# Block-sparse attention and expert routing on one core: gathered blocks interleaved over partitions 32 to 95

## The chip, the cores and the metric

The kernel runs on one core of one Trainium2 chip. A core has a matrix engine (TensorE, PE; its weight loads are PEld), three engines for elementwise work (VectorE or DVE, ScalarE or ACT, GpSimd or POOL), a queue engine that issues transfers (SyncE or SP), and 16 DMA engines. Its fast memory, SBUF, has 128 partitions; results of matrix multiplications go to PSUM. The metric is the device time in microseconds (us) of one execution. A profile is one further execution taken by the hardware profiler; its span runs from the first to the last instruction.

## What is computed

Sparse attention (4 batch entries, 8 heads, 768 positions, head size 64) is followed by a router that sends each token to one of 8 experts. Positions form 24 blocks of 32. A query block sees its own block and the two beside it, the first and the last block, and three blocks drawn at random for it. The first and last query blocks see everything.

```python
scores = scale * np.matmul(q, k.transpose(0, 1, 3, 2))
mask = np.abs(blk_i - blk_j) <= 1
mask = mask | (blk_i == 0) | (blk_j == 0) | (blk_i == n_blocks - 1) | (blk_j == n_blocks - 1)
for qb in range(n_blocks):
    for kb in sampled_blocks[qb]:
        mask[qb * block:(qb + 1) * block, kb * block:(kb + 1) * block] = True
attn = softmax(np.where(mask, scores, -1e9))
x = np.matmul(attn, v)                    # then to (3072 tokens, 512)
...
logits = normalized(x) @ normalized(expert_emb).T / tau
expert_idx = np.argmax(logits, axis=1)    # gate_w: its softmax probability
out[mask_e] = gate_w[mask_e, None] * (np.maximum(x[mask_e] @ w1[e], 0.0) @ w2[e])
```

All data are float32. The random block numbers are an input, so the kernel reads them on the device and uses them as addresses.

## The kernel before

**Stages.** Attention fills about the first 265 us. The rest is the experts: tiles of 128 tokens, whose rows are gathered by an indirect transfer and multiplied by `w1` (L1171) and `w2` (L1184), with 4 MB of weights for each tile.

**Attention.** Two batch entries are taken together (a pair, `DUO`), and the positions are cut into 6 chunks of 128, each with 4 query blocks, g = 0 to 3 (`NG`). One step of the loop in `attention_fast` (25 of them) handles one chunk of one batch entry. The order of the work on every engine is the order in which this loop writes it; no scheduler changes it. The loop is software-pipelined: in step s PE scores chunk s (`score_near`, `score_far`) and weighs the values of chunk s - 1 (`weigh_near`, `weigh_far`), DVE and POOL collect the keys of chunk s + 1 (`gather_k`), and SP issues the transfers of values for a later pair of chunks (`gather_v`).

**Near and far.** Keys that lie together (the window's own pair of blocks, and the first and last block) are multiplied where they are (`score_near`). Four further key blocks of each query block g are collected into one set of 128 lanes: the three random blocks, called slots 0, 1 and 2 (`NRAND`), and one neighbour block. In the keys' tile `kg` the lanes lie along the free dimension, so collecting is a copy within each partition. DVE copies slot 0 and the neighbour (L532, L536), POOL copies slots 1 and 2 (L532). PE then multiplies the lanes in two halves of 64 (L575), ACT takes the exponential with a bias for each lane (L580), which blanks a lane whose block is seen already, and the result `pd` has the lane as its partition. PE therefore needs the values of the same four blocks with the lane as partition, in the tile `vg` (L630). The three random slots of `vg` come from memory by transfers on SP, one for each slot and query block, for both batch entries and all heads at once: 32 rows of 16 pieces of 256 bytes, 128 KB (L469, issued in `fetch_all` at L476, L478 and L480). POOL copies the neighbour from the values that are in SBUF (L490). `vg` has two buffers, used by turns by pairs of chunks.

**Lanes before.** Slot r has lanes 32 r to 32 r + 31, and the neighbour has 96 to 127, in `kg`, `vg` and the bias alike. The bias, one number for each lane and query block, is built once near the start on DVE (`build_bias`, L351 to L370), between a copy of turned keys (L503) and the first collecting copies.

**Queues.** All loads of attention but three go through SP's one queue, in the order written: gathers (vg) with a load of q, k or v ahead of every other one, and the write of finished rows to `x_dram` (L834), from which the experts' tiles gather.

Of the kernel before, what the change touches and what calls it, by code (L numbers as in the profile page):

```python
# [12 lines left out]
F32 = mybir.dt.float32  # L13
I32 = mybir.dt.int32
BF16 = mybir.dt.bfloat16
ACT = mybir.ActivationFunctionType
ALU = mybir.AluOpType
# [3 lines left out]
P = 128  # L21
B, H, S, D = 4, 8, 768, 64
BLK = 32
NB = S // BLK
NRAND = 3
# [26 lines left out]
NI = NB - 2  # L52
# [6 lines left out]
NONE = -30000.0  # L59
# [28 lines left out]
def warm_up(k, times):  # L88

    if k.zeros is None:  # L90
        k.zeros = k.const.tile([P, 512], BF16, name="zeros")
        k.nc.vector.memset(k.zeros, 0.0)
        k.warm = two_banks(k, "warm")
    for i in range(times):
        k.nc.tensor.matmul(k.warm[:, 0], lhsT=k.zeros[:, 0:P], rhs=k.zeros, start=True, stop=True)
# [253 lines left out]
def build_bias(k):  # L349

    nc, pool, r = k.nc, k.setup, k.rand  # L351
    own = pool.tile([P, NI], F32, name="own_block")
    nc.gpsimd.iota(own, pattern=[[1, NI]], base=1, channel_multiplier=0, allow_small_or_imprecise_dtypes=True)
    bad = pool.tile([P, NRAND, NI], F32, name="bad_block")
    nc.vector.tensor_tensor(out=bad, in0=r, in1=own.unsqueeze(1).broadcast_to([P, NRAND, NI]), op=ALU.subtract)
    nc.vector.tensor_tensor(out=bad, in0=bad, in1=bad, op=ALU.mult)
    nc.vector.tensor_scalar(out=bad, in0=bad, scalar1=1.5, scalar2=None, op0=ALU.is_le)
    nc.vector.scalar_tensor_tensor(out=bad, in0=r, scalar=0.5, in1=bad, op0=ALU.is_le, op1=ALU.max)
    nc.vector.scalar_tensor_tensor(out=bad, in0=r, scalar=NB - 1.5, in1=bad, op0=ALU.is_ge, op1=ALU.max)
    for s, t in ((1, 0), (2, 0), (2, 1)):  # L360
        same = pool.tile([P, NI], F32, name=f"same{s}{t}")
        nc.vector.tensor_tensor(out=same, in0=r[:, s], in1=r[:, t], op=ALU.is_equal)
        nc.vector.tensor_tensor(out=bad[:, s], in0=bad[:, s], in1=same, op=ALU.max)
    k.bias = k.const.tile([P, NI], F32, name="bias")
    nc.vector.memset(k.bias, 0.0)
    for i in (0, NI - 1):
        nc.vector.memset(k.bias[NRAND * BLK:P, i:i + 1], NONE)
    for s in range(NRAND):
        lanes = slice(s * BLK, (s + 1) * BLK)
        nc.vector.tensor_scalar(out=k.bias[lanes], in0=bad[lanes, s], scalar1=NONE, scalar2=None, op0=ALU.mult)  # L370


def shifts(k, engine, s, c):

    blocks = blocks_of(c)
    key = engine, s, c
    if key not in k.shift:
        _, values = k.nc.values_load_multi_w_load_instructions(
            k.offset[0:1, s, NG * c + blocks[0]:NG * c + blocks[-1] + 1], engines=(engine,), min_val=0, max_val=S - BLK,
            skip_runtime_bounds_check_because="the block numbers are clamped to the blocks there are")  # L380
        if engine == mybir.EngineType.SP and s == NRAND - 1:
            return list(values)
        k.shift[key] = list(values)
    return k.shift[key]


def pair_chunk(s):

    a, at = divmod(s, NC)
    return a, at if a == 0 else (at + 1) % NC  # L390


def place(n):

    a, c = pair_chunk(n // DUO)
    return DUO * a + n % DUO, c, n % DUO


def of_seq(src, a, i=None):

    if i is None:
        return src[DUO * a:DUO * (a + 1)].rearrange("i h s d -> s (i h) d")
    return src[DUO * a + i].rearrange("h s d -> s h d")


def in_pair(t, i=None):

    return t.rearrange("p i h e -> p (i h) e") if i is None else t[:, i]
# [24 lines left out]
def which(i):  # L433

    return slice(0, DUO) if i is None else slice(i, i + 1)
# [15 lines left out]
def blocks_of(c):  # L451

    return range(2 if c == 0 else 0, NG)


def home(block):

    tile = (block + 1) // 2
    lo = (D if tile % 2 else 0) + BLK * (1 - block % 2)
    return slice(lo, lo + BLK), tile // 2  # L460


def gather_v(k, s, i=None):

    a, c = pair_chunk(s)
    t, src = k.vg_ring[s % 2], of_seq(k.v, a, i)
    for r in range(NRAND):
        for g, shift in zip(blocks_of(c), shifts(k, mybir.EngineType.SP, r, c)):
            yield in_pair(t[r * BLK:(r + 1) * BLK, g], i)[:, :, 0:D], src[bass.ds(shift, BLK)]  # L469


def fetch_all(k, gathers, loads):
# [10 lines left out]
def near_v(k, s, some, i=None):  # L483

    _, c = pair_chunk(s)
    for g in blocks_of(c):
        block = NG * c + g - 2 if g % 2 == 0 else NG * c + g
        if g in some and 0 < block < NB - 1:
            rows, m = home(block)
            k.nc.gpsimd.tensor_copy(out=k.vg_ring[s % 2][NRAND * BLK:P, g, which(i)], in_=k.vt[m][rows, which(i)])  # L490


def turn_k(k, g):
# [28 lines left out]
def gather_k(k, n):  # L522

    nc = k.nc
    b, c, _ = place(n)
    kt = k.kt[b % 2]
    k.kg[n] = t = k.gp.tile([P, NPAIR, NG, P], F32, name="kg", tag="kg")
    for s in range(NRAND):
        engine, copy = ((mybir.EngineType.Pool, nc.gpsimd.tensor_copy) if s else
                        (mybir.EngineType.DVE, nc.vector.tensor_copy))  # L530
        for g, shift in zip(blocks_of(c), shifts(k, engine, s, c)):
            copy(out=t[:, :, g, s * BLK:(s + 1) * BLK], in_=kt[:, :, bass.ds(shift, BLK)])  # L532
    for half in range(1 if c == 0 else 0, 2):
        for z in range(2):
            lo = BLK * (NG * c + 2 * half - 2 + 3 * z)
            nc.vector.tensor_copy(out=t[:, :, 2 * half + z, NRAND * BLK:P], in_=kt[:, :, lo:lo + BLK])  # L536


def score_near(k, n):
# [723 lines left out]
def attention_fast(n, ctx):  # L1263
# [3 lines left out]
    nc = n.nc  # L1267
# [26 lines left out]
        fetch_all(n, (), load_k(n, g))  # L1294
    load_experts(n)
    warm_up(n, 10)
    nc.vector.memset(n.vg_ring[0][NRAND * BLK:P, 2], 0.0)
    nc.scalar.activation(n.setup.tile([P, 1], F32, name="first_exp"), n.zeros[:, 0:1], ACT.Exp)
    build_ident(n)
    for i in range(2):  # L1300
# [3 lines left out]
    for vg in n.vg_ring:  # L1304
        nc.gpsimd.memset(vg[:, :, :, :, D:D + 1], 1.0)
    build_choice(n)
    fetch_all(n, gather_v(n, 0), [])
    for m in range(2, NC):
        fetch_all(n, (), load_v(n, 0, m, 0))
    turn_q(n, 0)  # L1310
    for g in range(NPAIR):
        turn_k(n, g)
        if g + 6 < 2 * NPAIR:
            fetch_all(n, (), load_k(n, g + 6))
    fetch_all(n, gather_v(n, 1), load_q(n, 0, 1) + load_q(n, 1, 1))
    for m in range(NC):
        fetch_all(n, (), load_v(n, 0, m, 1))
    build_bias(n)
    gather_k(n, 0)
    n.half = n.const.tile([P, NC], F32, name="half")  # L1320
    nc.vector.memset(n.half, 0.5)
    experts = build_experts(n)
    stack_ends(n, 0, (1,), 0)
    stack(n, 0, 0)
    near_v(n, 0, range(NG), 0)
    next(experts)
    zero = n.const.tile([1, XW], F32, name="zero")
# [8 lines left out]
    for s in range(NCH + 1):  # L1336
# [9 lines left out]
        def keys_gathered():  # L1346
            if after is not None:
                gather_k(n, after)
# [9 lines left out]
        if s == 0:  # L1358
            stack_ends(n, 1, (0, 1), 0)
            stack(n, 1, 0)  # L1360
            near_v(n, 1, range(NG), 0)
        elif s == 2:
            stack_ends(n, 0, (1,), 1)
            stack(n, 0, 1)
            near_v(n, 0, range(NG), 1)
        elif s == 3:
            stack_ends(n, 1, (0, 1), 1)
            stack(n, 1, 1)
            near_v(n, 1, range(NG), 1)
        elif s == 4:  # L1370
            stack_ends(n, 0, (0,))
            stack(n, 2)
        elif s % 2 and 5 <= s < NCH:
            if s // DUO + 1 in (NC, NC + 1):
                stack_ends(n, s // DUO + 1, (0, 1))
            stack(n, s // DUO + 1)
# [26 lines left out]
        ahead, odd = s // DUO + 1, s % DUO  # L1403
# [5 lines left out]
        if s == 3:  # L1409
            gathers = gather_v(n, ahead)  # L1410
        elif s >= 4 and ahead < NS:
            if not odd:
                coming = gather_v(n, ahead)
            gathers = coming if odd else islice(coming, 6)
# [104 lines left out]
def fast(n):  # L1519
    n.rings, n.loads = {}, 0  # L1520
    with ExitStack() as ctx:
# [6 lines left out]
        with ExitStack() as attn:  # L1528
            n.attending = True
            with n.tc.manual_schedule(engines=None):  # L1530
                attention_fast(n, attn)
            n.attending = False
# [137 lines left out]
```

## Time and profile before

| | us |
|---|---|
| three runs | 632.78, 636.43, 636.05; median 636.05 |
| profiled execution, its own time | 636.59 |
| its span | 634.9 |
| PE, PEld busy | 596.5 (94%), 455.6 (72%) |
| DVE, ACT, POOL busy | 233.9 (37%), 148.7 (23%), 244.0 (38%) |
| vg transfers (L478) | 132 of 128 KB |
| kg copies on POOL (L532) | 176, 43.2 busy, mean 290 ns |
| kg copies on DVE (L532, L536) | 88 and 88, medians 221 and 219 ns |

The page of a profile gives, for each engine, its busy time, and then the span in 40 equal slices, where a digit is the busy share in tenths, PEclk the granted share of the matrix engine's clock and DMA the share of the 16 DMA engines. A row of waits names the engine and line that waited, what ended the wait, the sum, how many there were, and the longest. "Issue" stands for time in which an engine waited for nothing that the profile shows. The chain of waits follows the work that ended last back from the end, each piece with its start and its length.

### The profile page before, as it was taken

What the parts mean: (1) busy time and instruction counts of PE and PEld (TensorE: products, weight loads), DVE (VectorE), ACT (ScalarE), POOL (GpSimd) and SP (SyncE); (2) the same over time, 40 slices, a digit from 0 to 9 for tenths busy, and PEclk for the clock granted to TensorE, in tenths of its full rate; (3) what the DMA queues carried; (4) which work ended last, traced back from release to release, by engine and by line L of the source; (5) the groups of instructions that cost most, each with busy time, mean ns of one, the idle gap of its engine ahead of it and who ended that gap; (6) DMA issues with size and microseconds to landing.
All of it is one profiled execution on the core that took longest, in us unless ns stands there. A gap on an engine that the chain in (4) does not pass through costs nothing.

```text
span 634.9 us, 18707 instructions
## 1 busy us (share of the span) xinstructions
PE 596.5 (94%) x7678; PEld 455.6 (72%) x7678; DVE 233.9 (37%) x740; ACT 148.7 (23%) x309; POOL 244.0 (38%) x473
## 2 busy tenths in 40 slices
PE   6889997898989998899999999999999999999995
PEld 3778886787878887767777776663777746667773
DVE  2535663666668862347511112112111131212110
ACT  1525563554555544210000000000000000000000
POOL 1716463544656631121134333333334433333432
PEclk9889998999999999999999999999999999999999
DMA  9999999999999992199999999999999998999611
GB/s 169 191 173 193 161 160 160 183 186 172 186 186 186 180 228 72 55 384 395 401 398 405 403 393 362 339 345 323 338 402 405 394 376 313 403 393 410 248 40 34
DMA packets 187312, 170.58 MB, mean 269 GB/s; under 512 B 147720, under 2 KB 147848, under 8 KB 184402
## 3 DMA queue, kind: packets, MB, share of 16 engines
q1 hardware_dynamic: 179906, 155.35, 87.4%
q0 software_dynamic: 5216, 13.43, 5.8%
q8 instruction: 62, 1.02, 0.8%
q10 hardware_dynamic: 2096, 0.52, 0.5%
q14 instruction: 32, 0.26, 0.2%
HBM read 156.65 MB, written 12.90 MB: 267 GB/s over the span
## 4 chain that ended last, share of the span: by engine, by line
PE 76%; DMA 9%; SPq 6%; issue 3%; ACT 2%; DVE 2%; POOL 1%; POOLq 0%; DVEq 0%; ACTq 0%
PE hp L1171 25%; PE yp L1184 24%; PE av L630 7%; PE dps L575 4%; DMA vg<-in_v_dram 4%; SPq L478 4%; PE ac L550 2%; PE hp L1216 2%; PE yp L1236 2%; DMA kraw<-in_k_dram 2%; PE ac L553 2%; DMA w<-in_moe_w_dram 2%; PE yp L514 2%; PE bps L606 1%; PE xg_ps L707 1%
## 5 line engine op out<-in xcount | busy, mean ns | idle before, releaser
L1171 PEld LDWEIGHTS hp<-xgt,w 128*128 128x128 f32 x1472 | 167.8, 192 | 11.3 <-issue 10.2
L1171 PE MATMUL hp<-xgt,w 128*128 128x128 f32 x1472 | 169.2, 275 | 0.8 <-DMA w<-in_moe_w_dram 0.8
L1184 PE MATMUL yp<-w,h 128*128 128x512 f32 x368 | 161.9, 592 | 0.0
L1184 PEld LDWEIGHTS yp<-w,h 128*128 128x128 f32 x368 | 68.1, 190 | 76.5 <-issue 75.8
L1095 POOL DMA_INDIRECT xg<-x_dram,quarter x88 | 89.2, 1014 | 32.3 <-issue 27.7
L1197 POOL DMA_INDIRECT out_dram<-y,slot_l x20 | 20.5, 1023 | 156.0 <-DVE y L1196 156.0
L1174 ACT ACTIVATE h<-hp 128x512 f32<-128x512 f32 x23 | 13.7, 597 | 284.1 <-PE hp L1171 240.4
L1178 DVE TENSOR_SCALAR h<-hp 128x512 f32<-128x512 f32 x23 | 15.9, 691 | 148.5 <-PE hp L1171 148.5
L490 POOL COPY vg<-vt 32x1040 f32<-32x1040 f32 (+1 forms) x45 | 42.9, 954 | 54.4 <-PE av L630 40.5
L532 POOL COPY kg<-kt 128x128 f32 x176 | 43.2, 290 | 35.9 <-ACT kt L503 31.3
L575 PEld LDWEIGHTS dps<-qt,kg 128*64 128x64 f32 x1408 | 47.5, 140 | 3.0 <-POOL vg L490 1.5
L575 PE MATMUL dps<-qt,kg 128*64 128x64 f32 x1408 | 46.9, 224 | 2.6 <-DVE kg L532 1.3
L550 PE MATMUL ac<-qt,kt 128*64 128x128 f32 x352 | 44.2, 277 | 3.6 <-issue 1.4
L1196 DVE TENSOR_SCALAR y<-yp,gate 128x512 f32<-128x512 f32 x20 | 15.0, 751 | 82.0 <-PE yp L1184 69.9
L519 DVE COPY qt<-yp 64x512 f32<-64x512 f32 x48 | 33.0, 688 | 32.1 <-PE yp L514 31.7
L553 PE MATMUL ac<-qt,kt 128*64 128x256 f32 (+1 forms) x192 | 43.4, 368 | 0.8 <-ACT kt L506 0.8
L630 PE MATMUL av<-vg,pd 128*32 128x65 f32 x1408 | 34.5, 227 | 7.6 <-DMA vg<-in_v_dram 5.4
L550 PEld LDWEIGHTS ac<-qt,kt 128*64 128x64 f32 x352 | 37.8, 137 | 5.2 <-issue 3.5
L580 ACT ACTIVATE pd<-dps,bias 128x256 f32<-128x256 f32 x88 | 34.7, 474 | 17.4 <-PE dps L575 17.4
L630 PEld LDWEIGHTS av<-vg,pd 128*32 128x32 f32 x1408 | 24.6, 111 | 17.5 <-issue 9.6
L630 PE MATMUL av<-st,pac 128*64 128x65 f32 x704 | 31.6, 226 | 2.9 <-DVE x L825 1.5
L630 PEld LDWEIGHTS av<-st,pac 128*64 128x64 f32 x704 | 25.7, 137 | 7.6 <-issue 6.5
(234 smaller groups left out, 608.0 us busy)
## 6 DMA issues: line engine op xcount, KB each, us to landing
w<-in_moe_w_dram SPq DMA_DIRECT2D x52, 2048.0 KB
vg<-in_v_dram SPq DMA_DIRECT2D x132, 128.0 KB
kraw<-in_k_dram SPq DMA_DIRECT2D x32, 192.0 KB
x_dram<-x SPq DMA_DIRECT2D x10, 516.0 KB
qraw<-in_q_dram SPq DMA_DIRECT2D x9, 512.0 KB
w<-in_moe_w_dram SPq DMA_DIRECT2D x8, 512.0 KB
vt<-in_v_dram SPq DMA_DIRECT2D x10, 256.0 KB
vt<-in_v_dram SPq DMA_DIRECT2D x5, 512.0 KB
```

The lines of the kernel that those rows point to most:

```text
L478: k.nc.sync.dma_start(out=to, in_=src)
L490: k.nc.gpsimd.tensor_copy(out=k.vg_ring[s % 2][NRAND * BLK:P, g, which(i)], in_=k.vt[m][rows, which(i)])
L519: k.nc.vector.tensor_copy(out=t[rows, :, h], in_=ps[rows])
L532: copy(out=t[:, :, g, s * BLK:(s + 1) * BLK], in_=kt[:, :, bass.ds(shift, BLK)])
L550: nc.tensor.matmul(out[0:D, j, half], lhsT=kt[:, j, at:at + D], rhs=qt[:, j, :, D * half:D * (half + 1)], start=True, stop=True)
L553: nc.tensor.matmul(out[D:P, j, half:2].rearrange("p f h t -> p h f t"), lhsT=kt[:, j, S:S + D], rhs=qt[:, j, :, D * half:P].rearrange("p h ...
L575: nc.tensor.matmul(out[D * r:D * (r + 1), NG * j + g], lhsT=kg[:, j, g, D * r:D * (r + 1)], rhs=qt[:, j, :, cols], start=True, stop=True)
L580: nc.scalar.activation(e[:, :, g].rearrange("p j h t -> p j (h t)"), out.rearrange("p (j g) h t -> p j g (h t)", g=NG)[:, :, g], ACT.Exp, ...
L630: k.nc.tensor.matmul(av[lanes, h // NPAIR, h % NPAIR * P:h % NPAIR * P + D + 1], lhsT=lhsT, rhs=rhs, start=first[0], stop=last, skip_group ...
L1095: k.nc.gpsimd.indirect_dma_start(out=x[:, g], out_offset=None, in_=quarters, in_offset=bass.IndirectOffsetOnAxis(ap=k.quarter[:, g, t:t + ...
L1171: nc.tensor.matmul(hp[:, f, :], lhsT=w1[:, d, (f0 + f) * P:(f0 + f + 1) * P], rhs=xt[:, d, :], start=(d == 0), stop=(d == ND - 1))
L1184: nc.tensor.matmul(yp, lhsT=h[:, f, :], rhs=w2[:, f, :], start=(f == 0), stop=(f == NF - 1))
```

## The change

The lanes are dealt out anew. Slots 0 and 1 share lanes 32 to 95: slot 0 has the even ones, slot 1 the odd ones. Slot 2 has lanes 0 to 31 where g is even and 96 to 127 where g is odd; the neighbour block has the other of the two. A new function, `lanes_of`, gives the lanes of a slot for a query block, and every place that named lanes calls it: the transfers of values, POOL's and DVE's neighbour copies, and the collecting copies of keys, in which slots 0 and 1 now write every other word. PE and ACT use the lanes as before. The bias is built for the new order: the two slots' numbers are merged by a lane's parity, which an iota on POOL provides.

```diff
@@ build_bias
     k.bias = k.const.tile([P, NI], F32, name="bias")
-    nc.vector.memset(k.bias, 0.0)
-    for i in (0, NI - 1):
-        nc.vector.memset(k.bias[NRAND * BLK:P, i:i + 1], NONE)
-    for s in range(NRAND):
-        lanes = slice(s * BLK, (s + 1) * BLK)
-        nc.vector.tensor_scalar(out=k.bias[lanes], in0=bad[lanes, s], scalar1=NONE, scalar2=None, op0=ALU.mult)
+    odd = pool.tile([P, 1], I32, name="odd")
+    nc.gpsimd.iota(odd, pattern=[[0, 1]], base=0, channel_multiplier=1)
+    nc.vector.tensor_scalar(out=odd, in0=odd, scalar1=1, scalar2=None, op0=ALU.bitwise_and)
+    odd_f = pool.tile([P, 1], F32, name="odd_f")
+    nc.vector.tensor_copy(out=odd_f, in_=odd)
+    nc.vector.tensor_tensor(out=bad[:, 1], in0=bad[:, 1], in1=bad[:, 0], op=ALU.subtract)
+    nc.vector.scalar_tensor_tensor(out=bad[:, 0], in0=bad[:, 1], scalar=odd_f[:, 0:1], in1=bad[:, 0], op0=ALU.mult,
+                                   op1=ALU.add)
+    nc.vector.tensor_scalar(out=k.bias, in0=bad[:, 0], scalar1=NONE, scalar2=None, op0=ALU.mult)
+    for g in range(2):
+        nc.vector.tensor_scalar(out=k.bias[lanes_of(2, g), g::2], in0=bad[lanes_of(2, g), 2, g::2], scalar1=NONE,
+                                scalar2=None, op0=ALU.mult)
+        nc.vector.memset(k.bias[lanes_of(NRAND, g), g::2], 0.0)
+        i = (NI - 1) * g
+        nc.vector.memset(k.bias[lanes_of(NRAND, g), i:i + 1], NONE)
+
+
+def lanes_of(slot, g):
+
+    if slot < 2:
+        return slice(BLK + slot, NRAND * BLK, 2)
+    return slice(0, BLK) if (slot + g) % 2 == 0 else slice(NRAND * BLK, P)
@@ gather_v
-            yield in_pair(t[r * BLK:(r + 1) * BLK, g], i)[:, :, 0:D], src[bass.ds(shift, BLK)]
+            yield in_pair(t[lanes_of(r, g), g], i)[:, :, 0:D], src[bass.ds(shift, BLK)]
@@ near_v
-            k.nc.gpsimd.tensor_copy(out=k.vg_ring[s % 2][NRAND * BLK:P, g, which(i)], in_=k.vt[m][rows, which(i)])
+            k.nc.gpsimd.tensor_copy(out=k.vg_ring[s % 2][lanes_of(NRAND, g), g, which(i)], in_=k.vt[m][rows, which(i)])
@@ gather_k
-            copy(out=t[:, :, g, s * BLK:(s + 1) * BLK], in_=kt[:, :, bass.ds(shift, BLK)])
+            copy(out=t[:, :, g, lanes_of(s, g)], in_=kt[:, :, bass.ds(shift, BLK)])
...
-            nc.vector.tensor_copy(out=t[:, :, 2 * half + z, NRAND * BLK:P], in_=kt[:, :, lo:lo + BLK])
+            nc.vector.tensor_copy(out=t[:, :, 2 * half + z, lanes_of(NRAND, z)], in_=kt[:, :, lo:lo + BLK])
@@ attention_fast
-    nc.vector.memset(n.vg_ring[0][NRAND * BLK:P, 2], 0.0)
+    nc.vector.memset(n.vg_ring[0][lanes_of(NRAND, 2), 2], 0.0)
```

## The prediction

> **What bounds the kernel now.** I read the page's slices first, then busy time and DMA rate by stretches, then the waits of the attention stage, then the chain of waits.
>
> Slices of the page:
>
> ```profile
> PE   6889997898989998899999999999999999999995
> PEclk9889998999999999999999999999999999999999
> DMA  9999999999999992199999999999999998999611
> GB/s 169 191 173 193 161 160 160 183 186 172 186 186 186 180 228 72 55 384 395 401 398 405 403 393 362 339 345 323 338 402 405 394 376 313 403 393 410 248 40 34
> ```
>
> A slice is 15.9 us. In the first 14 slices (attention, to about 230 us) PE and DMA are both near full, with DMA moving only 160 to 190 GB/s. From slice 18 (experts) PE is full and DMA moves about 400 GB/s. The change touches only attention; the experts' 343 us shift as a block. So the question is how much of attention PE loses to DMA.
>
> Stretches chosen by what is in flight: full-height loads of v, q and k at 52 to 58, almost only gathered blocks (vg) at 71 to 77 and 123 to 128; then the 3.4 us before and after two stalls. The columns are the stretch, its length, busy us of PE, PEld, DVE, ACT, POOL, granted clock, DMA share, GB/s:
>
> ```profile
> 52.00:58.00 6.00, 6.00 (x132) 5.60 (x125) 4.38 (x13) 3.32 (x9) 5.37 (x15) 1.00 1.03 217
> 71.00:77.00 6.00, 5.83 (x162) 4.97 (x159) 3.28 (x7) 4.54 (x10) 2.06 (x2) 1.00 1.10 144
> 123.00:128.00 5.00, 5.00 (x124) 4.89 (x123) 2.83 (x13) 2.43 (x6) 0.00 (x0) 1.00 1.16 154
> ...
> 34.40:37.80 3.40, 1.25 (x38) 1.11 (x38) 0.94 (x1) 0.37 (x1) 0.00 (x0) 1.00 0.93 179
> 37.80:41.20 3.40, 3.40 (x69) 2.93 (x57) 0.93 (x4) 0.95 (x3) 2.89 (x12) 0.50 1.00 179
> 95.90:99.30 3.40, 1.62 (x28) 1.05 (x23) 0.69 (x1) 3.31 (x6) 3.03 (x6) 0.99 1.33 137
> 99.30:102.70 3.40, 3.24 (x66) 2.62 (x70) 0.93 (x2) 0.24 (x1) 2.13 (x9) 0.50 1.31 135
> ```
>
> All descriptors here are 256 B, yet gathers run at about 149 GB/s where loads to 128 partitions run at 217. And after each of two long stalls the clock is granted at 0.50 for 3.4 us.
>
> Waits of the attention stage, 30 to 235 us:
>
> ```profile
> PEld av L630 <- DMA vg<-in_v_dram: 7.8, 14, 2.3
> PE av L630 <- DMA vg<-in_v_dram: 5.4, 7, 2.2
> PE kps L501 <- DMA kraw<-in_k_dram: 4.1, 3, 2.2
> PE av L630 <- DVE x L825: 1.5, 1, 1.5
> PE ac L550 <- DVE qt L519: 1.3, 1, 1.3
> ```
>
> PE stands 5.4 us on gathered blocks and 4.1 us on k, which queues behind them on the same ring. The PEld row is the same stalls seen from the weight load, not a second sum. The 1.5 us behind L825 is a DMA wait too: in the chain DVE waits for x_dram's write.
>
> The chain of waits, in order of time:
>
> ```profile
> 103.99 4.28 DMA x_dram<-x
> ...
> 113.84 6.70 DMA vg<-in_v_dram
> ...
> 147.38 4.86 DMA kraw<-in_k_dram
> ```
>
> So DMA waits of PE come to 5.4 + 4.1 + 1.5 = **11.0 us**. The two half-clock windows cost up to half of 3.4 us each, **3.4 us**.
>
> [...] No row of before shows a strided kg copy.
>
> **The change, part by part.**
>
> *Gathers of slots 0 and 1 (L469).* There are 132 vg transfers of 128 KiB (131 KB), a third for each slot; 88 change. Now 131 / 149 = 0.88 us each; at 217 GB/s 0.60, at the 206 GB/s of another full-height stretch (58 to 64) 0.64. I take 0.62: 88 x 0.26 = 23 us of DMA time given back over 210 us. Bounds: nothing, [...] and 25 us. Issue on SP is unchanged: same DMAs, same order.
>
> *Slot 2 (44 transfers)* [...] I take nothing.
>
> *What the 23 us buy.* DMA is off the path where it gets ahead of PE. In the stretch with most waits, 84 to 124 us, some 15 changed transfers give 15 x 0.26 = 3.9 us plus what their neighbours gain; the waits of PE there are 4.1 on vg and 1.5 behind x_dram, partly one delay carried on. Of the first k waits (2.9 us near 34) only six gathers lie in front, issued slowly by SP: I expect 0.7 back and leave 2.2. Of the other 11.0 - 2.2 = 8.8 I take three quarters, since a landing lags its issue by 4 to 7 us in the chain and ragged ends remain: 6.6 us. Of the half-clock windows the one at 99.3 goes with its stall (1.7), the one at 37.8 with even chance (0.85): 2.55. Gain 9.15 us. What is late next is PE itself, which was busy 197 of the 215 us from 20 to 235, and DVE's chain k, kg, qt at step 11.
>
> *kg slot 0 on DVE (L532, 88 copies, 128 words to every other word).* [...] I take 0.09 us: 8 us of DVE over the stage, where DVE was busy 129 of 215 us. A step ahead (8 us) covers it. Uncovered are the start (two copies before PE's first dps) and steps 10 to 12, whose gather follows k's turn: with the bias below, 1.2 us in all. Without cover it would be the whole 8.
>
> *kg slot 1 on POOL (88 copies of 290 ns).* Rows of 1040 and 520 words take 1048 and 615 ns, so 0.83 ns a word, 107 ns for 128. A strided write costs between nothing and that again: 0 to 9.4 us on POOL, busy 115 of 215 us, and PE never waited for a POOL kg copy. I take half, hidden; uncovered, 0.05 a copy, 0.2 a step.
>
> *Neighbour blocks (L490, L536)* go to other partitions, same sizes: nothing. Each half of dps now needs copies of three slots where the first half needed two; queued behind is the rest of dps, then av. All copies finish a step earlier; at the start the missing neighbour copy ends 0.3 us after the first dps and the next matmul needed it anyway.
>
> *Bias (L365 to L370).* Six DVE instructions, 1.15 us from 18.62 to 19.77, become eleven: two on 128x1 (0.17 each by the nearest rows), two of 0.2 and one of 0.2 on 128x22, two of 0.2 to 0.3 and four memsets of 0.07, 1.4 to 1.9 us. Plus 0.3 to 0.7 us ahead of the first kg copy, on the path to PE's first dps; counted in the 1.2. The added iota runs on POOL while it stands idle 13.8 us until 17.55; DVE's wait on it is free.
>
> **Sum.** 9.15 - 1.2 = 7.95. The profiled execution took 636.59 us (span 634.9 and 1.7 around it), 0.54 above the median of 636.05: 636.6 - 8.0 = 628.6, and I forecast **628.5**.
>
> **Rivals.**
>
> *Hidden anyway.* DMA gets faster, but the stage keeps other waits: PE is 92% busy, DVE was busy 17 of 20 us at 200 to 220, and stalls shown as "issue" stay. Then only the vg waits, half of the x_dram and k ones and no clock go: 5.4 x 0.6 + 1 - 1.2 = 3.0; 633.5. For it: from 160 us on PE hardly waits for DMA. Against: before that, it does, and k and x_dram share the queue.
>
> [...] A gather has half the descriptors of a 128-row load of one batch entry, so a fixed cost a transfer could explain 0.88 too. Then nothing is gained, and DVE's start adds 1.2: 637.8. Against: k loads of 192 KB, hardly larger, run at 206 GB/s at 58 to 64, with q.
>
> *More.* Neighbours of the gathers (k and q in mixed stretches) also speed up, all 11.0 and 3.4 go: 636.6 - 14.4 + 1.2 = 623.4.
>
> *Slower: the interleaved write costs more than the plain one.* Place: the 88 transfers in a ring that is always full. From 0.88 + 0.073 us each (88 x 0.073 = 6.4) the stage is 1% of the kernel longer; at 110 GB/s, 1.19 us, it is 88 x 0.31 = 27 us of DMA of which perhaps 18 reach PE: 654. Nothing in the trace shows a write to every other partition; against it, its descriptors keep size and number.
>
> **How the numbers follow.** Forecast, 624 to 631: 0.50; more, 620 to 624: 0.10; hidden, 631 to 636: 0.20; [...] slower: 0.08. A measurement of this kernel can tell about 1% from no change: 629.7 and 642.4. Faster by over 1%: 0.46 of the forecast's 0.50 and the 0.10, 0.56. Slower: 0.08. Within: 0.36. The range leaves out most of the slower case, the worse half of no effect and a little of more: 621.5 to 638.
>
> **What would show it.** Right: vg-only stretches at 190 GB/s or more; PE's waits on vg under 2 us; full clock at 99; kg on DVE at 0.3 us or so, PE not waiting for it; experts unchanged in length. Wrong: gathers still near 150 GB/s [...]; gathers faster but attention ends as late (another wait); kg over 0.4 us with PE waits on L532.

## The result, and the profile after

The kernel after takes 628.81 us (median of four runs, 626.4 to 630.59), beside 636.12 for the kernel before (632.78 to 636.43): a ratio of 0.9887, 95% interval 0.9844 to 0.993, so between 4.5 and 9.9 us less. The forecast was 628.5. The profiled execution after took 626.4 us with a span of 624.7. It was a short one, 2.4 us under its median, while the profiled one of before was 0.5 over its own: some 3 us of the 10.2 us between the two traces is this luck.

Lines below L370 moved down by 16: L478 is now L494 (gathers), L532 L548 and L536 L552 (kg), L575 L591 (dps), L630 L646 (av), L501 L517 (kps), L825 L841 (x), L1171 L1187.

The slices of the page of after, 15.6 us each:

```profile
PE   6789998989999997999999999999999999999995
PEclk9789999999999999999999999999999999999998
DMA  9889888999987971599999999998999998999611
GB/s 167 171 184 193 180 174 180 195 195 208 202 183 186 190 222 37 179 372 399 399 407 398 393 397 365 333 318 305 385 408 398 396 381 308 400 394 410 241 35 34
```

Attention ends earlier: the dip in DMA before the experts (37 GB/s) is one slice long and comes in slice 16. DMA has 8s in attention, so it is no longer always full, and yet in slices 2 to 14 it moves 171 to 208 GB/s where it moved 160 to 193. The first expert matmul starts at 257.1 us, beside 267.9; what follows it, 367.6 us, is as long as before (367.0). All of the gain lies in attention.

Stretches of after, with the columns of the prediction: the full-height loads, the two stretches of gathers, and 3.4 us each at the start of dps, after the wait for k, at 99.3 us, and at 249 us:

```profile
52.00:58.00 6.00, 6.00 (x160) 5.54 (x149) 4.96 (x13) 3.00 (x8) 5.58 (x15) 1.00 1.00 215
71.00:77.00 6.00, 5.83 (x170) 4.97 (x168) 3.21 (x9) 4.85 (x9) 1.62 (x2) 1.00 0.83 171
123.00:128.00 5.00, 5.00 (x126) 4.10 (x124) 3.74 (x12) 2.61 (x6) 0.41 (x1) 1.00 0.92 194
...
20.50:27.30 6.80, 4.79 (x45) 4.70 (x46) 4.31 (x22) 3.11 (x7) 4.35 (x13) 0.50 0.66 145
37.60:41.00 3.40, 3.31 (x54) 2.83 (x56) 0.92 (x4) 1.30 (x3) 0.89 (x4) 0.50 0.87 190
99.30:102.70 3.40, 3.22 (x64) 3.06 (x64) 0.88 (x3) 0.80 (x3) 2.44 (x9) 1.00 0.74 172
249.10:252.50 3.40, 3.40 (x64) 3.11 (x67) 0.00 (x0) 0.00 (x0) 0.00 (x0) 0.51 0.02 5
```

Full-height loads run as before (215 against 217 GB/s). The stretches of gathers went from 144 to 171 and from 154 to 194 GB/s, at a DMA share of 0.83 and 0.92 instead of 1.10 and 1.16: faster, and with time to spare. The clock is full at 99.3 us, but half at 37.6, at 249 and, for 6.8 us, at the start.

PE's waits of after, 30 to 235 us:

```profile
PE ac L566 <- DVE qt L535: 2.7, 2, 1.4
PE av L646 <- DVE x L841: 2.4, 1, 2.4
PE kps L517 <- DMA kraw<-in_k_dram: 2.0, 1, 2.0
```

The row of vg, 5.4 us before, is gone. Of three waits for k the longest is left (2.2 us at 36.6 before, 2.0 at 37.7 now). The wait behind x_dram grew from 1.5 to 2.4, the one for qt from 1.3 to 2.7. In the chain of waits of 20 to 240 us seven pieces of DMA have become two: k at 32.2 us and x_dram at 100.5.

### The profile page after: what moved, and what is told of

The parts are those of the page before. It is cut to its first block, busy times and chain, and to the rows that moved or that the text cites. A ratio compares the mean times of both kernels' runs of the same rounds, so it can differ in the third digit from the quotient of the medians.

```text
span 624.7 us, 18708 instructions
## 1 busy us (share of the span) xinstructions
PE 591.9 (95%) x7678; PEld 454.1 (73%) x7678; DVE 236.1 (38%) x745; ACT 148.0 (24%) x309; POOL 244.1 (39%) x474
## 4 chain that ended last, share of the span: by engine, by line
PE 82%; ACT 5%; DMA 3%; DVE 2%; issue 2%; POOL 1%; SPq 0%; DVEq 0%; POOLq 0%; ACTq 0%
PE hp L1187 25%; PE yp L1200 24%; PE av L646 8%; PE dps L591 6%; PE ac L566 3%; PE ac L569 3%; PE hp L1232 2%; PE yp L1252 2%; DMA w<-in_moe_w_dram 2%; ACT st L458 2%; ACT pd L596 2%; PE xg_ps L723 2%; PE yp L530 1%; PE xg_ps L752 1%; ACT pb L624 1%
## 5 line engine op out<-in xcount | busy, mean ns | idle before, releaser
L1187 PEld LDWEIGHTS hp<-xgt,w 128*128 128x128 f32 x1472 | 167.8, 192 | 11.9 <-issue 10.2
L1187 PE MATMUL hp<-xgt,w 128*128 128x128 f32 x1472 | 169.2, 276 | 1.4 <-DMA w<-in_moe_w_dram 1.4
L548 POOL COPY kg<-kt 128x128 f32 x176 | 43.7, 296 | 35.1 <-ACT kt L519 31.1
L591 PEld LDWEIGHTS dps<-qt,kg 128*64 128x64 f32 x1408 | 47.2, 140 | 3.4 <-issue 3.4
L591 PE MATMUL dps<-qt,kg 128*64 128x64 f32 x1408 | 46.3, 224 | 3.2 <-DVE kg L548 3.2
L566 PE MATMUL ac<-qt,kt 128*64 128x128 f32 x352 | 43.9, 277 | 3.0 <-DVE qt L535 2.7
L566 PEld LDWEIGHTS ac<-qt,kt 128*64 128x64 f32 x352 | 37.8, 137 | 4.2 <-issue 3.2
L646 PE MATMUL av<-st,pac 128*64 128x65 f32 x704 | 31.2, 226 | 4.1 <-DVE x L841 3.4
L646 PEld LDWEIGHTS av<-st,pac 128*64 128x64 f32 x704 | 25.6, 138 | 8.6 <-issue 7.6
L646 PE MATMUL av<-vg,pd 128*32 128x65 f32 x1408 | 30.0, 225 | 1.8 <-issue 1.8
L725 DVE COPY xt<-xg_ps 128x512 f32<-128x512 f32 x24 | 16.6, 691 | 35.6 <-PE xg_ps L723 35.6
```

The lines of the kernel that those rows point to most:

```text
L548: copy(out=t[:, :, g, lanes_of(s, g)], in_=kt[:, :, bass.ds(shift, BLK)])
L566: nc.tensor.matmul(out[0:D, j, half], lhsT=kt[:, j, at:at + D], rhs=qt[:, j, :, D * half:D * (half + 1)], start=True, stop=True)
L591: nc.tensor.matmul(out[D * r:D * (r + 1), NG * j + g], lhsT=kg[:, j, g, D * r:D * (r + 1)], rhs=qt[:, j, :, cols], start=True, stop=True)
L646: k.nc.tensor.matmul(av[lanes, h // NPAIR, h % NPAIR * P:h % NPAIR * P + D + 1], lhsT=lhsT, rhs=rhs, start=first[0], stop=last, skip_group ...
L1187: nc.tensor.matmul(hp[:, f, :], lhsT=w1[:, d, (f0 + f) * P:(f0 + f + 1) * P], rhs=xt[:, d, :], start=(d == 0), stop=(d == ND - 1))
```

## The experiments

Each run is compared with runs of the kernel before on the same chip; rows with the same time of before shared it. "First expert" is the start of the first expert matmul, in us, in the one profile of each kernel; the runs came from several chips, on which the kernel before had medians from 633.9 to 636.1, so a difference of 2 us in this column says little.

| run | median us | before there | ratio (95%) | first expert |
|---|---|---|---|---|
| before, after | 636.12, 628.81 | | 0.9887 (0.9844 to 0.993) | 267.9, 257.1 |
| e1_same_half | 637.36 | 633.93 | 1.0028 (0.9999 to 1.0058) | 269.5 |
| e2_slot2_fixed | 629.38 | 633.93 | 0.9898 (0.9852 to 0.9944) | 259.9 |
| e3_plain_spread | 631.5 | 633.93 | 0.9953 (0.9934 to 0.9972) | 263.4 |
| e4_bias_late | 631.04 | 633.93 | 0.9947 (0.9915 to 0.9979) | 260.0 |
| e6_before_no_slot2 | 659.34 | 633.98 | 1.0393 (1.0351 to 1.0435) | 254.6 |
| e7_after_no_slot2 | 660.17 | 633.98 | 1.0402 (1.0362 to 1.0442) | 253.1 |
| e10_bias_early | 628.25 | 633.98 | 0.9893 (0.985 to 0.9937) | 259.7 |
| e11_bias_early_k_first | 628.33 | 633.98 | 0.9911 (0.9889 to 0.9933) | 262.0 |
| e12_slot2_act | 638.48 | 636.09 | 1.0042 (1.0022 to 1.0062) | 269.5 |
| e13_e11_slot2_act | 634.85 | 636.09 | 0.9988 (0.9966 to 1.001) | 263.4 |
| e14_x_pool | 629.44 | 634.38 | 0.9907 (0.9872 to 0.9941) | 258.2 |
| e15_x_act | 646.62 | 634.38 | 1.0171 (1.0134 to 1.0208) | 277.1 |

### Is it the place of the partitions? Interleaved, but in one half

```diff
 def lanes_of(slot, g):
     if slot < 2:
-        return slice(BLK + slot, NRAND * BLK, 2)
-    return slice(0, BLK) if (slot + g) % 2 == 0 else slice(NRAND * BLK, P)
+        return slice(slot, 2 * BLK, 2)
+    return slice(slot * BLK, (slot + 1) * BLK)
```

> Slots 0 and 1 interleaved on even and odd partitions 0 to 63 instead of 32 to 95; slot 2 on 64 to 95 and the neighbour on 96 to 127 for every g. Same strides, same number of instructions, [...]. Theory [...]: the gain is lost; vg-only stretches move 140 to 160 GB/s, PE waits on vg by 4 to 8 us again, and the start of the change (1.9 us more before the first dps) stays: 635 to 640. Rival (any placement that isn't 32 adjacent rows helps, or the gain comes from other waits): 627 to 631, vg stretches as in the changed kernel (184 GB/s), no waits on vg.

The strides, the longer bias and the kg copies into every other word are all there; what differs is the place. Slots 0 and 1 interleave on 0 to 63, and slot 2 and the neighbour lie where the kernel before has them, on 64 to 95 and 96 to 127. It takes 637.36 us, 0.3% above the kernel before. Its stretch of gathers, and then PE's wait on them from 30 to 235 us:

```profile
71.00:77.00 6.00, 6.00 (x182) 5.30 (x180) 3.29 (x12) 4.98 (x9) 0.42 (x1) 1.00 1.03 143
```

```profile
PE av L646 <- DMA vg<-in_v_dram: 6.5, 7, 2.2
```

The 144 GB/s and the waits of before are back (5.4 us there). So the runs part the change into two terms: going from one half of the partitions into both is worth 1.4%, about 9 us, give or take 3 by the two intervals, and all the rest of the change costs 0.3%, 1.8 us at the middle of its interval, nothing to 3.7 at its ends.

### Does slot 2's alternation carry any of it?

```diff
     if slot < 2:
         return slice(BLK + slot, NRAND * BLK, 2)
-    return slice(0, BLK) if (slot + g) % 2 == 0 else slice(NRAND * BLK, P)
+    return slice(0, BLK) if slot == 2 else slice(NRAND * BLK, P)
```

> The changed kernel, but slot 2 always on partitions 0 to 31 and the neighbour block always on 96 to 127, so only the interleaving is left. Theory [...]: alternating a 32-row transfer between halves changes nothing much, 627.5 to 631, waits on vg below 1.5 us. Rival (balance of the two halves over successive transfers carries part of the gain): 631.5 to 635, with 2 to 4 us of waits on vg.

Slot 2 always lies on 0 to 31 and the neighbour on 96 to 127. The ratio is 0.9898 beside 0.9887: no difference that can be measured.

Beside the run before it, this one settles more. Both send two thirds of the gathered bytes to the lower half of the partitions and one third to the upper: there slots 0 and 1 lie low and slot 2 high, here half of the rows of slots 0 and 1 lie low, half high, and slot 2 low. On the same chip they took 637.36 and 629.38 us. So it is not how the queue as a whole divides between the halves that makes these 8 us, but that each interleaved transfer reaches both.

### And whole transfers on alternate halves, without interleaving?

```diff
     if slot < 2:
-        return slice(BLK + slot, NRAND * BLK, 2)
+        return slice(BLK * (slot + 1), BLK * (slot + 2))
```

The parity that merges the bias becomes "lane 64 or above" in the same number of instructions.

> No interleaving: slot 0 on 32 to 63, slot 1 on 64 to 95, slot 2 and the neighbour by turns on 0 to 31 and 96 to 127, so both halves get equal bytes but each transfer still goes to 32 adjacent rows (the bias is built with as many instructions, by a shift of the lane number in place of its parity). Theory [...]: each transfer keeps 0.88 us, 635 to 639, waits on vg 4 to 8 us; SP issues a gather in 316 ns at least, as before. Rival (balance over transfers): 628 to 632, waits on vg under 2 us.

Slot 0 has 32 to 63 and slot 1 has 64 to 95, each whole, so that both halves get as many transfers. The ratio is 0.9953: of the 1.4% between one half and both this gives 0.75%, about half, with the same bias. The theory of the expectation missed; its rival met the time, but not the waits. The stretch of gathers, and PE's wait on them from 30 to 235 us:

```profile
71.00:77.00 6.00, 5.82 (x141) 4.97 (x138) 4.40 (x15) 4.56 (x10) 3.09 (x5) 1.00 1.01 172
```

```profile
PE av L646 <- DMA vg<-in_v_dram: 3.4, 8, 0.8
```

172 GB/s in this stretch, where the run with two thirds of the transfers in the lower half gave 143. The waits are about as many as before (8 beside 7), but the longest is 0.8 us and not 2.2. The rate of one stretch doesn't rank the kernels: the kernel after has 171 GB/s here, and the one with slot 2 fixed 160, though both take less time. What does rank these five is how long PE is busy with the 1408 matmuls that read `vg` ("av<-vg,pd" on each page): 35.5 us with the interleaving in one half, 34.5 before, 33.1 here, 30.8 with slot 2 fixed and 30.0 after.

### How much do transfers hold attention at all?

```diff
-    for r in range(NRAND):
+    for r in range(NRAND if s < 3 else NRAND - 1):
```

> The kernel before, in which the gathers of values leave out random slot 2 from the fourth pair of chunks on: 34 of 132 transfers of 128 KB are not made, and the old values in those lanes are used. Theory (before, the attention stage loses about 8 us to a DMA ring that is always full): 34 x 0.88 = 30 us of DMA fall away, more than the 23 us which the change gives back, so the waits on vg and behind x_dram go, and the kernel takes 625 to 628 us, ratio 0.987. Rival (the gain of the change came from somewhere else than from transfers that finish sooner, such as the order of DVE's work): ratio above 0.995.

> The kernel after with the same 34 transfers of random slot 2 left out (old values are used in those lanes). Theory (after the change transfers bound almost nothing; what is left are one wait for k near 36 us, before the first transfer that is left out, and one behind x_dram near 104 us): under 2 us less than the kernel after, ratio to the kernel before 0.986 to 0.989. Rival (the gathers still hold the stage back, now by the time that SP takes to issue a strided one, 0.6 us against 0.32): another 3 to 5 us go, ratio under 0.983.

The whole times missed, because of something that the expectations had not thought of: the old values change x, and with it the experts that tokens go to, 24 tiles instead of 23 (1536 matmuls of the kind hp and not 1472), with a wait of some 17 us of PE near the end. Attention does the same work on PE, so its end can be read, where the first expert matmul starts. The rows of that line, kernel before and kernel after, each without the 34 transfers:

```profile
L1171 PE MATMUL hp<-xgt,w x1536: 272/275/552, 254.6 to 640.6; 128*128 128x128 f32 x192
```

```profile
L1187 PE MATMUL hp<-xgt,w x1536: 272/275/550, 253.1 to 639.1; 128*128 128x128 f32 x192
```

The kernel before gains 267.9 - 254.6 = 13.3 us, the kernel after 257.1 - 253.1 = 4.0. Moved by how far each profiled execution lay from its own median, these become some 15 and 6, an estimate. With 34 transfers fewer both layouts end attention within 1.5 us of each other. So transfers cost the kernel before at least some 13 to 15 us, and the change took some 8 to 11 of them (10.8 between the two traces, 3 of which may be luck). For the kernel after the rival was right: 4 to 6 us of transfers, or of their issue, were left.

### Does the longer bias cost what it shows?

PE's gap ahead of its first dps grew from 1.3 to 3.2 us. Two of the added instructions on DVE took 0.64 us each, where the prediction took 0.2. The columns are start and length in us:

```profile
19.10 0.64 DVE L371 SCALAR_TENSOR_TENSOR bad_block<-bad_block,odd_f 128x22 f32<-128x22 f32 x1
19.78 0.64 DVE L373 TENSOR_SCALAR bias<-bad_block 128x22 f32<-128x22 f32 x1
```

POOL at the same time:

```profile
19.10 0.62 POOL L464 COPY st<-vt 64x520 f32<-64x520 f32 x1
19.77 0.61 POOL L506 COPY vg<-vt 32x520 f32<-32x520 f32 x1
```

Each of the two ran just while POOL made a copy. In the runs with the bias late and early, where POOL runs nothing beside them, the same two take 0.24 and 0.18 us. DVE's read of the block numbers for the first kg copies (L378 before, now L394, 0.77 us) also moved: it ran beside the bias from 18.8 us, and now starts behind it, at 21.2. The first kg copy starts at 22.1 us and not 19.8.

Three runs moved the bias.

```diff
-    build_bias(n)
     gather_k(n, 0)
+    build_bias(n)
```

> The changed kernel with build_bias after gather_k of chunk 0 instead of ahead of it, so DVE's first kg copies don't stand behind the eleven bias instructions. Theory (the start costs the changed kernel 1.9 us of PE time: its gap before the first dps is 3.17 us against 1.30): the gap falls under 1 us, 625 to 627.5. Rival (the start is given back at the wait for k near 36 us, which DMA sets): 628 to 629.5 and a longer wait for k.

The gap before the first dps went, and DVE's copy of k, now behind the bias, kept PE 3.3 us (row "PE ac L566, DVE kt L519"): the same cost one place later. The ratio, 0.9947, is no better than that of after, and neither of the two expectations was met.

```diff
     turn_q(n, 0)
     for g in range(NPAIR):
+        if g == 2:
+            build_bias(n)
         turn_k(n, g)
...
-    build_bias(n)
     gather_k(n, 0)
```

> The kernel after with the whole building of the bias moved ahead of the third of four turns of k, where DVE waits 3.8 us for PE, so that it no longer stands before the first collecting copies. Theory (the longer bias costs 1.9 us at the start, but the start is covered by the wait for k near 36 us, which does not depend on it): PE's wait before its first dps falls from 3.2 us to 1 or less, the wait for k grows from 2 to about 4 or 5 us, and the whole gains under 1 us: ratio to the kernel before 0.987 to 0.990. Rival (the start is paid in full): 2.5 us or more less than the kernel after, ratio 0.984.

Here the bias stands where DVE waits for PE in any case. PE's waits of this kernel, 15 to 235 us:

```profile
PE kps L517 <- DMA kraw<-in_k_dram: 4.7, 2, 3.4
PE ac L566 <- DVE qt L535: 3.8, 2, 2.5
PE av L646 <- DVE x L841: 1.8, 1, 1.8
PE dps L591 <- issue: 1.2, 1, 1.2
```

The 3.2 us on kg are gone, the wait for k grew from 2.0 to 4.7, that for qt from 2.7 to 3.8, and the ratio is 0.9893, as expected: what the start lost had been covered by these waits.

```diff
-    for m in range(2, NC):
+    for m in range(2, 4):
         fetch_all(n, (), load_v(n, 0, m, 0))
...
             fetch_all(n, (), load_k(n, g + 6))
+    for m in range(4, NC):
+        fetch_all(n, (), load_v(n, 0, m, 0))
```

> As the run before it, and the loads of k for the third pair of heads' turn in step 1 (four transfers) go ahead of the last two loads of v of the first batch entry on SP. Theory (the wait for k near 36 us is the time that SP takes to issue what stands before it, 0.8 to 1.2 us each, and not the speed of the transfers): k lands some 2.4 us sooner, the wait for k falls to 3 us or less, and the kernel takes 2 to 3 us less than the kernel after: ratio 0.984. Rival (the later loads of v then make POOL and PE wait as long): same as the kernel after, 0.988.

With the bias early and these loads of k ahead of two of v, the matmuls that waited for k go on at 34.5 us instead of 37.3, as the theory had it. But the whole gains nothing (628.33 us): the rival. The wait behind x_dram is 3.8 us in this profile, and vg waits of 1.2 us are there, as in the run before. What the first 36 us gained was given back later.

### What is left: SP's pace, or the write to x_dram?

SP's issue of a strided gather turned out to take longer: 596 ns at the shortest in the first of the two kernels below, beside 316 ns for a gather to 32 adjacent partitions in the kernel before. These next two kernels moved slot 2's 44 gathers to ACT, the second one with the early bias and k first.

```diff
-        for g, shift in zip(blocks_of(c), shifts(k, mybir.EngineType.SP, r, c)):
-            yield in_pair(t[lanes_of(r, g), g], i)[:, :, 0:D], src[bass.ds(shift, BLK)]
+        engine, queue = ((mybir.EngineType.SP, k.nc.sync) if r < 2 else
+                         (mybir.EngineType.Activation, k.nc.scalar))
+        for g, shift in zip(blocks_of(c), shifts(k, engine, r, c)):
+            yield queue, in_pair(t[lanes_of(r, g), g], i)[:, :, 0:D], src[bass.ds(shift, BLK)]
```

> The kernel after with the 44 gathers of slot 2 issued by ACT instead of SP, in the same places of the program. Theory (after the change the gathers are spaced by SP, which takes 0.6 us to issue a strided one and some 0.84 from one to the next, and no longer by the DMA engines, whose share is below 1): a third of the issues off SP lets the transfers run ahead, the wait behind x_dram near 104 us falls below 1 us, the first expert matmul starts 2 to 4 us sooner than in the kernel after (257.1 us), and the ratio to the kernel before is 0.983 to 0.986. Rival (what is left after the change is not SP's pace; the transfers or the chain k, kg, qt hold it, or ACT loses as much by issuing): 0.988 or more.

> The run before it, together with the bias built ahead of the turns of k and with the four loads of k ahead of two loads of v (the kernel of the run with k first). Theory (the first 36 us gained nothing by themselves because SP's pace gave it back by 105 us; with SP relieved they count): 1 to 3 us less than with slot 2 on ACT alone, ratio 0.979 to 0.983. Rival (the later part is paced by something else): the same as with slot 2 on ACT alone.

The first kernel's issues apart, strided ones on SP and adjacent ones on ACT (shortest, median and longest in ns):

```profile
L496 SPq DMA_DIRECT2D vg<-in_v_dram x88: 596/597/2772, 22.1 to 231.0; - x88
...
L496 ACTq DMA_DIRECT2D vg<-in_v_dram x44: 322/334/1289, 6.9 to 226.4; - x44
```

Neither gained: 638.48 us is 0.4% above the kernel before, 634.85 level with it. The second took 3.6 us less than the first, so the early bias and k first did count here. What held both up is to be read in SP's waits, of the first one from 60 to 115 us:

```profile
SPq L496 <- DMA vg<-in_v_dram: 13.4, 4, 7.2
```

With the gathers on two queues, SP waits for the end of gathers, of which its waits before and after (30 to 235 us) have none; the second kernel has 38.4 us of such waits. In the first the stretch of 60 to 80 us then runs at 138 GB/s, below before's 166, and PE waits 6.8 us behind x_dram and 5.8 for k, whose transfers SP issues. ACT too waits 8.9 us for gathers there, where after has no such wait; how much of the loss is ACT's was not separated. So the pair does not tell what SP's pace costs; they measured waits that the edit brought in, and why the program has them was not tried.

Then the write of finished rows. In after, x is ready at 94.5 us, its write is issued at 99.9, behind gathers and loads of k on SP, and DVE waits 5.4 us for it to land.

```diff
-        nc.sync.dma_start(out=dram[lo:lo + rows.stop - rows.start], in_=...)
+        nc.gpsimd.dma_start(out=dram[lo:lo + rows.stop - rows.start], in_=...)
```

> The kernel after with the ten writes of finished rows to x_dram issued by POOL instead of SP. Theory (the largest wait that the change left in the middle, 2.4 us of PE near 104 us, is not the speed of the transfer: x is ready at 94.5 us, SP issues its write at 99.9 us, behind seven strided gathers and two loads of k, and it lands at 105.6 us): issued from POOL's own queue the write goes at about 95 to 97 us, PE's wait on DVE x falls below 0.5 us, and the ratio to the kernel before is 0.984 to 0.987. Rival (the time comes back as another wait within the stage, or POOL's copies are held up by the issue): 0.988 or more.

> As the run before it, with the writes issued by ACT. Theory: the same wait goes and the same is gained, ratio 0.984 to 0.987, unless ACT's wait for DVE ahead of the write (SP waited up to 3.3 us at one of them) holds up the exponentials that PE needs: then 0.990 or more, with PE waits on ACT of 1 us and longer. Rival: the wait behind x_dram goes and PE waits as long for gathers, since these now have the queue to themselves no sooner: 0.988.

From POOL the wait goes, and another takes its place. PE's waits of that kernel, 90 to 125 us:

```profile
PE av L646 <- DMA vg<-in_v_dram: 3.6, 2, 3.2
PE av L646 <- DVE x L841: 0.6, 1, 0.6
```

2.4 us on x became 0.6, and 3.6 us on gathers came 10 us later, where after had none. The whole is at 0.9907, within the interval of after: the rival. From ACT it is worse than the kernel before, and not because PE waits for ACT, as the expectation had allowed: PE waits 10.3 us for gathers, and SP again waits across queues (30 to 275 us):

```profile
SPq L494 <- DMA x_dram<-x: 35.3, 6, 10.6
```

## Why the prediction was right, point by point

**The step from one half of the partitions into both held; what makes it was not shown.** That an interleaved transfer would take 0.62 us and not 0.88 was the author's estimate, from the 206 and 217 GB/s of full-height loads beside the 149 of gathers. The run with the same strides in one half (143 GB/s from 71 to 77 us, beside 171 in the kernel after) shows that the place of the partitions, not the stride, the size or the order, makes the 9 us; with slot 2 fixed, the same division of the bytes between the halves still gains 8 of them. The rival of no gain (636 to 640 us, given 0.12) and "slower" are refuted. No trace shows by what mechanism the place counts.

**The gain, 9.15 us taken and about 9 measured, was right in its waits and lucky in the rest.** The waits of 30 to 235 us fell by 5.4 us on vg and by 2.1 on k (3.0 us between 33 and 37 became 2.0, where 2.2 was the guess, and one of 1.2 near 152 went). The wait behind x_dram, which was to shrink, grew by 0.9. That is 6.6 us net, as much as was taken. The 2.55 us for the clock did not come, and some 4.5 us came that no term of the sum had: the two next points. That these nearly make up for each other is luck. The e14 run suggests that x_dram's wait and the gathers' are one delay that moves between them; one profile shows it.

**The clock was mis-sized: 2.55 us taken, nothing net.** The window at 99 us went with its stall as forecast. But the one at 37.8 stayed, a second one came beside that at 20.8, where the gap had grown, and one came at 249; the mean clock from 20 us to the first expert matmul fell from 0.98 to 0.97. A window was 3.4 us long again (0.50 from 37.6 to 41.0 us). The length of the gap does not decide it: in the kernel after PE stood 2.0 us ahead of the window at 37.6 us and 1.8 us ahead of the one at 249, but 2.4 us ahead of 106.5, where the clock stayed full (1.00 from 106.4 to 109.8 us). What does decide it was not shown, and a forecast should not count on a window.

**Where the clock's share came from instead.** The same 5576 matmuls, from 20 us to the first expert matmul, first before, then after:

```profile
20.00:267.90 247.90, 224.64 (x5576) 197.31 (x5577) 139.61 (x496) 126.98 (x269) 117.53 (x322) 0.98 1.00 167
```

```profile
20.00:257.10 237.10, 220.06 (x5576) 195.67 (x5576) 141.75 (x503) 126.33 (x269) 117.65 (x322) 0.97 0.81 174
```

10.8 us shorter: 6.2 less in which PE stood, and 4.6 less in which it counted as busy, at a clock that is no better. The pages show where the 4.6 lie. The matmuls that read the gathered blocks, before and after (busy us, mean ns of one, then the idle time before them):

```profile
L630 PE MATMUL av<-vg,pd 128*32 128x65 f32 x1408 | 34.5, 227 | 7.6 <-DMA vg<-in_v_dram 5.4
```

```profile
L646 PE MATMUL av<-vg,pd 128*32 128x65 f32 x1408 | 30.0, 225 | 1.8 <-issue 1.8
```

As many matmuls, each as long as before, took 4.5 us less: before, they followed each other at greater distances, too short to show as idle time, since matmuls overlap in the profile (1408 of 227 ns in 34.5 us). With the interleaving in one half these 1408 are at 35.5 us again, and without the 34 transfers at 30.1 in the old layout and 30.3 in the new. So late gathers cost PE 5.4 us in its row of waits and some 4.5 in work that only looked busy. The reading that PEld's row is "not a second sum" left out a part of this: it has 14 waits and 7.8 us where PE's has 7 and 5.4. The 13 to 15 us of the runs without 34 transfers, beside 11.0 us of waits in the prediction, say the same.

**The cost, 1.2 us taken, lies within what was measured (1.8 us, but nothing to 3.7 by its interval), and was wrong in its parts.** "Plus 0.3 to 0.7 us ahead of the first kg copy" was 2.3 us, and 1.9 of PE's wait: the two instructions that met POOL's copies, and the read of block numbers that came out from beside the bias. The early bias took it away and gained nothing that can be measured. The strided kg copies cost 8 ns on DVE (median 229 beside 221 ns, 0.09 us taken). On POOL the mean of all 176 rose from 290 to 296 ns; as half of them are strided, some 12 ns each by estimate (0.05 us taken). The 0.09 and the 0.05 us were the author's estimates; no trace of before had such a copy.

**"Issue on SP is unchanged: same DMAs, same order" failed.** The count and the order are the same, the time of one is not: 596 ns at the shortest for every other partition, beside 316 ns for 32 adjacent ones in the kernel before. The stretches of gathers show it from the other side: at 71 us the DMA share fell to 0.83 while the rate stayed at 171 GB/s, short of the 190 that was to show the step right and that the stretch at 123 us met (194, at 0.92). Before, at a share of 1.10 and 1.16, SP's pace did not show. What it is worth was not settled.

**"I take nothing" for slot 2 held** (0.9898 beside 0.9887), **but whole transfers by turns on the two halves are not worth nothing everywhere.** With them dealt evenly over both halves the gathers of 71 to 77 us ran at 172 GB/s, against 143 where two thirds of them lay in one half, 20% more, and the kernel gained half of what interleaving gives. That slot 2's alternation adds nothing because its neighbours in the queue reach both halves already is the author's guess, and was not shown.

**The rival "hidden anyway"** was right that other waits are left (k, x, qt: 7.1 us of PE), and wrong that they hold the gain back. The chain to qt, named as late next, is now PE's longest row, 2.7 us.

None of these kernels beats the kernel after by more than the measurement's width; the early bias (628.25 us) is level with it.

## What to carry to other kernels

Where many transfers to few partitions fill the ring, as here those to 32 partitions (DMA shares of 1.10 and 1.16 at 144 and 154 GB/s), try dealing their rows over both halves of the partitions, within one transfer if the layout can be chosen freely, and by turns between transfers if it can't: here the one gave 1.1% and the other 0.5%. Read a transfer-bound stage by the place where its work ends, with some transfers left out, and by the busy time of the matmuls that read what is transferred, not by the sum of its waits alone: here nearly half of what late gathers cost counted as busy (4.5 of 9.9 us), and a wait taken away singly came back as another. Look at what the other engine does while an instruction is slow (here 0.64 us while POOL copied, 0.24 and 0.18 while it was idle). Before a queue is relieved by issuing on a second engine, look at what the first one then waits for.

## What was unexpected of the hardware

- Issuing a transfer of 32 rows to every other partition took at least 596 ns on SP (slot 2 on ACT), to adjacent partitions at least 316 on SP (the kernel before) and 322 on ACT, with the same pieces of 256 bytes.
- Two DVE instructions on 128x22 elements took 0.64 us each while POOL copied 64x520 and 32x520 elements, and 0.24 and 0.18 us with POOL idle. No run moved POOL's copies alone.
- A copy into every other word cost 4% on DVE (229 beside 221 ns) and, by the estimate above, some 4% on POOL.
- Issues moved from SP to ACT came with waits between queues: with slot 2's gathers on ACT, SP waited 13.4 us for the end of gathers from 60 to 115 us, and with x on ACT 35.3 us for the end of its writes from 30 to 275 us. Time was lost, not saved: ratios to the kernel before of 1.0042 and 0.9988 with gathers on ACT, 1.0171 with x on ACT, where the kernel after has 0.9887.
